# ScalarE's order in the second layer of a fused convolution and gated MLP

## The chip, the cores and the metric

The kernel runs on one core of one Trainium2 chip. The metric is the device time of one execution in microseconds (us), given as the median of several runs. The engines are named as in the profile: PE is TensorE (matmuls; its weight loads are listed as PEld), ACT is ScalarE, DVE is VectorE, POOL is GpSimd, and SP is the engine that only issues DMAs here.

## The reference, cut to what matters

```python
def _attn_ref(x, weight):                      # x: 8 x 4096 x 192, weight: 8 heads x 7 taps
    w = softmax(weight)                        # over the 7 taps
    x_pad = np.concatenate([np.zeros((B, 6, D)), x], axis=1)
    x_unf = x_pad[:, idx, :].reshape(B, S, K, H, group)
    return np.einsum('hk,bskhg->bshg', w, x_unf).reshape(B, S, D)

def _moe_ref(x, w_in, w_out):                  # 32768 x 192, 192 x 2048, 2048 x 192
    h = x @ w_in
    g = h * np.clip(h + 3.0, 0.0, 6.0) / 6.0
    return g @ w_out
```

The result y of the convolution goes through the first layer (`x @ w_in`), the gate, and the second layer (`g @ w_out`). All is float32.

## The kernel before, in words

**Blocks.** The 32768 tokens are cut into 32 blocks (NB) of 1024, each of two halves of 512. Block 0 is done in a plainer way beside the preparation of the weights. Blocks 1 to 31 run in a loop (lines 1116 to 1134): `first_layer(i)`, then `second_layer(i)`. Beside the second layer of block i the kernel prepares the next blocks: it loads x of block i+2, starts its convolution (two of the seven taps), and splits y of block i+1 into three parts that the first layer reads: `split_high` (ACT, line 476), `split_low` (DVE, line 1081), `split_mix` (DVE, line 479). The parts are then swapped between the two halves of the partitions by six DMAs on POOL's queue (`swap_parts`, lines 266 and 267).

**Second layer as seven products.** The gated values `g` are held as a 2x2 matrix of blocks (A11, A21, A12, A22) and `w_out` as B11 to B22. The product is formed by Strassen's scheme in Winograd's form: seven products P1 to P7 of sums of A blocks (S1 to S4) and of B blocks (T1 to T4), which are then added up. In two of the three output thirds of some products the same scheme is used once more on quarters ("level two", `small` and `level_two`), with matmuls of 256 columns instead of 512.

**Four streams.** A matmul here uses 32 of PE's 128 columns. Four streams (j = 0 to 3), one for each group of 32 columns and so for the 32 partitions `rows(j)` of PSUM, run side by side. Each stream is a list of matmuls laid on a clock by hand (`put`): a matmul of 512 columns costs 2 steps, one of 256 costs 1 step, and every stream ends at step 80 (line 814). All other work of the layer is put on the same clock by `do(t, ...)`: a job with time t is written out after all matmuls that begin by then. At the end all jobs and matmuls are sorted by their times and issued in that order (line 910). So the times fix only the order on each engine, in which the engine then works strictly; what a job waits for is found by the framework, which adds the semaphores.

**What the streams hold.** Stream 3 (fourth column group) is made of 56 matmuls of 256 columns (level two of P1 and of P5) and 12 of 512: four of P2 and eight that `fill` puts in, P5's third third into rows 96 to 127 of the PSUM bank b. `fill` runs at steps 4, 36, 48 and 76. Stream 0 holds P4's third third (steps 0 to 16, into `b[first]`, rows 0 to 31), later at step 44 P6 on top of P1 in the same bank, and at step 64 P3.

**The jobs that the change and the prediction touch**, all inside `second_layer`:

- `p4[third, t]` <- `b[first, t]` (lines 816, 817): ACT copies P4's third third out of PSUM in two halves of 256 columns. In the trace these are L650 COPY `shared<-psum` 32x256 x2.
- `b[m]` <- `p1` (line 848): ACT writes P1 into PSUM bank b, where P6 is then added to it by matmuls: P1's seed. In the trace: L650 COPY `psum<-z` 96x512.
- `negative(pair)` (lines 713, 714 and 851, 852): S4 = A12 - S2 for two of the eight chunks, four pairs in all. ACT writes -S2 into S3's place (L572 ACTIVATE `s<-g`), then POOL issues a DMA that adds A12 to it in memory (`adding`, line 569, `s<-g`). P3 reads the pairs (0,2), (1,3), (4,6), (5,7) at steps 64, 68, 72 and 76. A fifth job of the same kind, `last_sum`, writes into `sums2` (`z<-z`).
- `split_high` (put at 48.4, line 1126): the rounding of y, L476 ACTIVATE `y_own<-y`. `split_low` (57) reads it.
- `late["p7"]` <- `c[m]` (line 853, at 56.5), then on DVE `late["u3"]` = `b[m]` + `late["p7"]` (line 854, at 60.2; L458). The add reads bank b before P3 overwrites it at step 64.

Of the kernel before, what the change touches and what calls it, by code (L numbers as in the profile page):

```python
# [25 lines left out]
def kernel(  # L26
# [61 lines left out]
    for base, dma in ((0, nc.scalar), (D2, nc.sync)):  # L88
        dma.dma_start(  # L89
            out=w_sb[base : base + D2],  # L90
            in_=weight.unsqueeze(1).to_broadcast([H, GJ, KC]),
# [126 lines left out]
    for n in range(AHEAD):  # L218
# [8 lines left out]
        out=e_sb[:], in0=w_sb[:], in1=mx[:].to_broadcast([P, KC]), op=ALU.subtract  # L227
# [53 lines left out]
    def take():  # L281
        return free_banks.pop(0)
# [163 lines left out]
    def rows(q):  # L446
        return slice(q * QS, (q + 1) * QS)
# [20 lines left out]
    m = slice(0, DH)  # L468
# [116 lines left out]
    chunk_pairs = [slice(n, n + 3, 2) for n in (0, 1, 4, 5)]  # L585
# [35 lines left out]
    def second_layer(i, between):  # L621
        last = i + 1 == NB
        ours = [free_slots.pop(0) for _ in range(3)]
        x_, b, y_, c, a, _ = (psum[:, 2 * n + k] for n in ours for k in range(2))
        z = pools[1].tile([P, NP + 1, N], F32, name="z2", tag="other")
        sums2, p1 = z[:, 0:NP], z[0:DH, NP]
        ends = [psum[:, 2 * free_slots[0] + k] for k in range(2)] if last else [b, b]
        s5 = A22
        copy = nc.scalar.copy
        m = slice(0, DH)  # L630
        lo, hi = halves
        both = nc.sync, nc.scalar
        first, second, third, fourth = (rows(q) for q in range(4))
# [15 lines left out]
        def do(t, fn, *args, **kw):  # L649
            streams[3].append((t - 0.5, lambda: fn(*args, **kw)))  # L650
# [87 lines left out]
        p4 = Fourth()  # L738
# [75 lines left out]
        assert clock == [80] * 4  # L814

        for t in halves:
            do(35.1 if t == hi else 35, copy, out=p4[third, t], in_=b[first, t])
        do(25.5, copy, out=p1[third], in_=b[second])
        do(20, copy, out=B2, in_=A2)
        do(31.9, copy, out=C2, in_=B2)  # L820
# [24 lines left out]
        do(36.15, small_sums, s5, S1, (3,), nc.vector)  # L845
        do(36.2, small_sums, s5, S1, (2,), nc.vector)
        do(36.05, fold_with, p4, 2)
        do(40 if last else 38.7, copy, out=b[m], in_=p1)
        do(21, last_sum, sums2, A12)
        do(36.4, small_sums, s5, S1, (1, 4), nc.vector)  # L850
        for r, t in zip(chunk_pairs, (30.5, 39.7, 42.1, 48.3)):
            do(t, negative, r)
        do(56.5, lambda: copy(out=late["p7"], in_=c[m]))
        do(60.2, lambda: add(late["u3"], b[m], late["p7"]))
# [83 lines left out]
    with tc.manual_schedule():  # L938
# [4 lines left out]
            out=c_sb[:], in0=e_sb[:], in1=sm[:].to_broadcast([P, KC]), op=ALU.mult  # L943
# [14 lines left out]
        b = take()  # L958
        for _ in range(3):

            nc.tensor.matmul(
                out=psum[:, b], lhsT=zeros[:, 0:P], rhs=zeros[:], start=True, stop=True
# [59 lines left out]
        for slot, (c, group) in enumerate(parts):  # L1022
            first = slot < len(early)
# [88 lines left out]
        last = ctx.enter_context(tc.tile_pool(name="last", bufs=1, reuse_waits="tile"))  # L1112
# [3 lines left out]
        for i in range(1, NB):  # L1116
            jobs = {n: [tap] for n, tap in zip((-1, 1, 3, 5, 7), taps)}
            jobs[-1] = left + jobs.get(-1, [])
            first_layer(i, jobs)
            def begin_conv():  # L1120
                x_tiles[i + 2] = load_x(i + 2)
                conv[:] = conv_jobs(i + 2)

            between, conv = [], []
            if i + 1 < NB:
                between += [(48.4, split_high), (57, split_low), (70, split_mix)]
                between += [
                    (t, lambda n=n: swap_parts(nc.gpsimd, (n,)))
                    for n, t in ((HIGH, 69), (LOW, 69), (MIX, 71))
                ]  # L1130
            if i + 2 < NB:
                between += [(1, begin_conv), (61.5, lambda: conv[0]()), (62, lambda: conv[1]())]
            left = second_layer(i, between)
            taps = conv[2:]
# [33 lines left out]
```

## Time and profile before

| | |
|---|---|
| median of 3 runs | 2226.67 us (2226.42 to 2227.29) |
| the profiled execution's own time | 2226.7 us |
| its span in the trace | 2224.9 us |
| busy: PE, DVE, ACT, POOL | 100%, 89%, 78%, 53% of the span |
| granted PE clock over the span | 0.999 |
| first layer, block 3 (168.06 to 201.03 us) | 32.97 us: PE 32.97, DVE 29.92, ACT 30.97, POOL 23.93 busy |
| second layer, block 3 (201.03 to 236.40 us) | 35.37 us: PE 35.37, DVE 31.69, ACT 23.28, POOL 13.29 busy |

How to read it: the span runs from the first to the last instruction in the trace, and the execution's own time is 1.8 us longer. The busy time of PE is a union of matmul records, which overlap in time and whose ends are modelled, so that PE can be named busy while one of the four streams stands still. Each float32 matmul of the second layer shows as two records, one behind the other in the same column group.

### The profile page before, as it was taken

Reading aid. Unit: us, or ns where it says so; the run is one execution under the profiler, and the core shown is the slowest. Engines: PE = TensorE matmul, PEld = TensorE weight load, DVE = VectorE, ACT = ScalarE, POOL = GpSimd, SP = SyncE. Lnnn points to the kernel's source line nnn. Section 1 sums busy time; section 2 is a strip of 40 time slices with the busy share of each in tenths; the row PEclk is TensorE's granted clock in tenths of the full one; section 3 lists DMA queues with packets and bytes.
Section 4 is the critical chain, followed back from the end, with each engine's and each line's share of the span. In section 5 each row is a group of like instructions: output and inputs, shape, how many; then the busy total and the mean of one; then the engine's idle time right before and its main releaser. Section 6 shows DMA issues by size and latency. Waiting matters only on the chain.

```text
span 2224.9 us, 55392 instructions
## 1 busy us (share of the span) xinstructions
PE 2216.5 (100%) x22984; PEld 1516.6 (68%) x22984; DVE 1985.6 (89%) x1983; ACT 1738.1 (78%) x2391; POOL 1182.2 (53%) x1033
## 2 busy tenths in 40 slices
PE   9999999999999999999999999999999999999998
PEld 5467776677766676766777667776667776677766
DVE  8889998889898899988999988989889998899877
ACT  7478787787877878877878778787787887787876
POOL 2456644565544565445655456554456644556544
PEclk9999999999999999999999999999999999999999
DMA  6277778777778777787777877777877778777777
GB/s 157 61 135 144 144 145 150 138 142 146 144 137 160 134 144 138 145 155 131 143 148 144 145 145 141 146 140 143 155 135 144 138 148 153 132 144 144 132 140 119
DMA packets 353308, 313.20 MB, mean 141 GB/s; under 512 B 212480, under 2 KB 265216, under 8 KB 353056
## 3 DMA queue, kind: packets, MB, share of 16 engines
q0 software_dynamic: 114976, 234.46, 58.8%
q1 hardware_dynamic: 236840, 74.93, 16.7%
q8 instruction: 180, 2.95, 0.6%
q14 instruction: 72, 0.59, 0.1%
q10 hardware_dynamic: 1240, 0.27, 0.1%
HBM read 31.72 MB, written 25.17 MB: 26 GB/s over the span
## 4 chain that ended last, share of the span: by engine, by line
PE 99%; DVE 0%; ACT 0%; DMA 0%; SPq 0%; issue 0%; DVEq 0%; ACTq 0%
PE psum L653 49%; PE psum L511 46%; PE psum L296 2%; PE psum L341 2%; DMA x<-in_x_dram 0%; DVE shared L458 0%; DVE shared L464 0%; SPq L100 0%; SPq L133 0%; DVE top L175 0%; PE psum L953 0%; DVE y L255 0%; SPq L89 0%; ACT y L967 0%; ACT scale L186 0%
## 5 line engine op out<-in xcount | busy, mean ns | idle before, releaser
L653 PE MATMUL psum<-g,w_out 128*32 128x512 f32 (+1 forms) x5968 | 825.0, 503 | 0.3 <-ACT psum L650 0.3
L653 PE MATMUL psum<-s,w_out 128*32 128x512 f32 (+1 forms) x3024 | 710.5, 586 | 0.0
L306 DVE SCALAR_TENSOR_TENSOR g<-g,psum 128x1024 f32<-128x1024 f32 (+1 forms) x528 | 618.7, 1185 | 91.4 <-ACT g L302 90.8
L302 ACT ACTIVATE g<-psum,half 128x1024 f32<-128x1024 f32 (+1 forms) x528 | 565.2, 1087 | 6.0 <-PE psum L511 5.1
L653 PEld LDWEIGHTS psum<-g,w_out 128*32 128x32 f32 x5968 | 370.8, 110 | 254.5 <-issue 91.6
L511 PE MATMUL psum<-y_own,w_in 64*128 64x512 f32 x4464 | 523.3, 389 | 0.0
L511 PE MATMUL psum<-y_other,w_in 64*128 64x512 f32 x4464 | 516.0, 386 | 0.0
L523 ACT ACTIVATE psum<-psum 128x1024 f32<-128x1024 f32 x465 | 468.7, 1008 | 48.1 <-PE psum L511 45.5
L511 PEld LDWEIGHTS psum<-y_own,w_in 64*128 64x128 f32 x4464 | 413.5, 184 | 117.7 <-issue 26.0
L511 PEld LDWEIGHTS psum<-y_other,w_in 64*128 64x128 f32 x4464 | 418.1, 184 | 87.8
L603 POOL TENSOR_TENSOR shared<-g,shared 128x256 f32<-128x256 f32 x248 | 357.6, 1442 | 72.6 <-DVE g L306 41.4
L1058 DVE SCALAR_TENSOR_TENSOR y<-x,c_sb,y 128x1536 f32<-128x1536 f32 x186 | 335.3, 1803 | 1.5 <-ACT y L1056 1.4
L569 POOL DMA_DIRECT2D s<-g x124 | 148.4, 1197 | 283.5 <-ACT s L572 282.6
L653 PE MATMUL psum<-g,w_s 128*32 128x256 f32 x1488 | 287.0, 379 | 0.0
L653 PEld LDWEIGHTS psum<-s,w_out 128*32 128x32 f32 x3024 | 198.4, 110 | 77.3 <-issue 16.2
L569 POOL DMA_DIRECT2D g<-g x124 | 181.7, 1530 | 104.4 <-DVE s L414 104.4
L653 PE MATMUL psum<-z,w_out 128*32 128x256 f32 x992 | 232.8, 380 | 0.0
L653 PE MATMUL psum<-z,w_s 128*32 128x256 f32 x992 | 227.5, 379 | 0.0
L603 POOL TENSOR_TENSOR shared<-g 128x256 f32<-128x256 f32 x124 | 92.0, 742 | 166.8 <-DVE g L306 166.8
L266 POOL DMA_DIRECT2D y_other<-y_own x90 | 47.9, 532 | 238.3 <-PE psum L653 223.6
L650 ACT COPY psum<-psum 32x512 f32<-32x512 f32 x186 | 82.9, 446 | 116.7 <-PE psum L653 113.7
L653 PEld LDWEIGHTS psum<-g,w_s 128*32 128x32 f32 x1488 | 135.3, 110 | 52.7
(115 smaller groups left out, 2970.0 us busy)
## 6 DMA issues: line engine op xcount, KB each, us to landing
y_other<-y_own POOLq DMA_DIRECT2D x180, 384.0 KB, 8.1
g<-g POOLq DMA_DIRECT2D x124, 512.0 KB, 6.1
s<-g POOLq DMA_DIRECT2D x124, 512.0 KB, 6.7
z<-g POOLq DMA_DIRECT2D x62, 512.0 KB, 7.5
out_dram<-shared SPq DMA_DIRECT2D x378, 64.0 KB, 4.1
x<-in_x_dram SPq DMA_DIRECT2D x53, 388.5 KB, 5.7
z<-g SPq DMA_DIRECT2D x31, 512.0 KB, 3.3
stage<-in_moe_w_in_dram SPq DMA_DIRECT2D x16, 192.0 KB, 4.3
```

The costliest lines, as they stand in the source:

```text
L266: dma.dma_start(out=to[D2:P], in_=part[0:D2])
L296: nc.tensor.matmul(out=psum[:, b], lhsT=w[r], rhs=src, start=start, stop=stop, skip_group_check=onto,)
L302: nc.scalar.activation(r6, h, ACT.Relu, bias=half[:], scale=1.0 / 6.0)
L306: nc.vector.scalar_tensor_tensor(out=g_, in0=g_, scalar=1.0, in1=h, op0=ALU.min, op1=ALU.mult)
L341: lambda p=p: nc.tensor.matmul(out=bank[j * QS : (j + 1) * QS, tokens], lhsT=w_out[:, p, w, cols], rhs=x[:, p, tokens], start=(first and p ...
L511: nc.tensor.matmul(out=psum[:, 2 * slots[n] + k], lhsT=r32(w_in_parts[part][r, c, s]), rhs=r32(y_other[0][r, part, s] if group else y_own[ ...
L523: nc.scalar.mul(both(n), both(n), 4097.0)
L569: nc.gpsimd.dma_start(out=out, in_=x, accum_op=ALU.add)
L603: engine.tensor_tensor(out=o, in0=p, in1=q, op=op)
L650: streams[3].append((t - 0.5, lambda: fn(*args, **kw)))
L653: nc.tensor.matmul(out=out, lhsT=w, rhs=x, start=start, stop=True, tile_position=(0, j * QS), skip_group_check=True,)
L1058: jobs.append(lambda k=k: nc.vector.scalar_tensor_tensor(out=y[:], in0=x[:, :, k : k + N], scalar=c_sb[:, k : k + 1], in1=y[:], op0=ALU.mu ...
```

## The change

Two sets of times on the hand-laid clock are altered; no instruction is added or taken away.

```diff
         for t in halves:
-            do(35.1 if t == hi else 35, copy, out=p4[third, t], in_=b[first, t])
+            do(30 if t == hi else 29, copy, out=p4[third, t], in_=b[first, t])
         do(25.5, copy, out=p1[third], in_=b[second])
...
-        do(40 if last else 38.7, copy, out=b[m], in_=p1)
+        do(39.55 if last else 38.7, copy, out=b[m], in_=p1)
         do(21, last_sum, sums2, A12)
         do(36.4, small_sums, s5, S1, (1, 4), nc.vector)
-        for r, t in zip(chunk_pairs, (30.5, 39.7, 42.1, 48.3)):
+        for r, t in zip(chunk_pairs, (34.3, 36.3, 42.1, 52)):
             do(t, negative, r)
```

On ACT the order of a block (all but the last) becomes as follows; what is not named keeps its place.

| before | after |
|---|---|
| L744, **negation (0,2)**, L650 (256), L650 (512), **P4's two copies**, L748 x2, **seed**, L744, L650, **negation (1,3)**, L824, negation (4,6), L826, L827, L743, L650, **negation (5,7)**, **rounding of y**, L745, L853 (P7) | L744, **P4's two copies**, L650 (256), L650 (512), **negation (0,2)**, L748 x2, **negation (1,3)**, **seed**, L744, L650, L824, negation (4,6), L826, L827, L743, L650, **rounding of y**, **negation (5,7)**, L745, L853 (P7) |

In the last block there is no rounding of y: there negation (1,3) and the seed move ahead of L650 and L824, and negation (5,7) moves behind L745. The orders on PE, DVE, POOL and SP are the same as before. One wait of PE moves: the second `fill` (step 36) waited for the second of P4's copies; now only the P2 matmul at step 40 behind it has a wait for ACT there, for the copy L650 (512).

## The prediction, made before the changed kernel was run

> **What bounds the kernel now.** I read the chain of waits first, then PE's starts inside one second layer, then ACT and DVE beside them. The chain of waits names PE for 99% of the span and repeats every 68.33 us (lines from block 2 and 3, columns start, us, what):
>
> ```profile
> PE 99%; DVE 0%; ACT 0%; DMA 0%; SPq 0%; issue 0%; DVEq 0%; ACTq 0%
> ```
>
> ```profile
> 168.06 32.98 PE psum L511 x288
> 201.03 35.37 PE psum L653 x293
> 236.40 32.97 PE psum L511 x288
> ```
>
> That PE is busy without a gap does not mean that its streams are. In the second layer the starts of one stream's records show its pace: 0.429 us for 512 columns (234.90, 235.33, 235.76) and 0.216 us for 256 (228.27, 228.49). The timeline of PE in block 3 breaks that pace twice (start, us, what, xcount):
>
> ```profile
> 216.45 0.66 PE L653 MATMUL psum<-s,w_out 128*32 128x512 f32 x2
> 216.66 0.38 PE L653 MATMUL psum<-z,w_out 128*32 128x256 f32 x1
> 216.88 0.66 PE L653 MATMUL psum<-s,w_out 128*32 128x512 f32 x2
> 217.06 0.62 PE L653 MATMUL psum<-g,w_out 128*32 128x512 f32 x1
> ...
> 228.49 0.81 PE L653 MATMUL psum<-g,w_out 128*32 128x256 f32 x3
> 229.30 0.63 PE L653 MATMUL psum<-s,w_out 128*32 128x512 f32 x3
> 229.32 0.62 PE L653 MATMUL psum<-g,w_s 128*32 128x256 f32 x2
> ```
>
> Hold A: the `g` record at 217.06 is the second `fill` of stream 3. The last `shared` record of that stream began at 216.31, so it was due at 216.53: stream 3 is 0.53 late. Streams 1 and 2 (the `s` records) go on at their pace. Hold B: at 229.30 all four streams begin together, at P3 (step 64), while the ones that were on time (start 228.05, 0.43 long) had been done at 228.48. The list of waits says what ended each (us in total, times, longest):
>
> ```profile
> PEld psum L653 <- DVE shared L458: 14.3, 30, 0.5
> PEld psum L653 <- ACT shared L650: 13.1, 31, 0.4
> ```
>
> Each comes once per block: A is P4's copies, B is the add u3, which must read bank b before P3 overwrites it. Who made these late is in the timelines of ACT and DVE:
>
> ```profile
> 214.36 1.05 ACT L572 ACTIVATE s<-g 128x1024 f32<-128x1024 f32 x1
> 215.44 0.92 ACT L650 COPY psum<-psum 32x256 f32<-32x256 f32 x2
> 216.38 0.62 ACT L650 COPY shared<-psum 32x256 f32<-32x256 f32 x2
> 217.03 0.37 ACT L748 COPY z<-psum 32x256 f32<-32x256 f32 x1
> ...
> 219.00 0.59 ACT L650 COPY psum<-z 96x512 f32<-96x512 f32 x1 [1.22 <-PE psum L653]
> ...
> 224.29 1.06 ACT L572 ACTIVATE s<-g 128x1024 f32<-128x1024 f32 x1
> 225.26 1.48 ACT L476 ACTIVATE y_own<-y 128x1536 fp32r<-128x1536 f32 x1
> ```
>
> ```profile
> 226.77 1.76 DVE L1081 TENSOR_TENSOR y_own<-y,y_own 128x1536 fp32r<-128x1536 f32 x1 [1.82 <-ACT y_own L476]
> ...
> 228.56 0.69 DVE L458 TENSOR_TENSOR shared<-psum,shared 96x512 f32<-96x512 f32 x1
> ```
>
> P4's copies stand behind a negation; ACT then idles 1.22 us ahead of the seed, and from 219.00 on works without a pause up to the rounding of y, for which DVE idles 1.82 us; split_low and u3 follow on DVE back to back, and B ends with u3 at 229.25.
>
> **The change part by part.** No work is added or removed, and POOL's DMAs keep their order, so only places count. I lay ACT's new order out with its own rows; the spacing of one to the next is 1.08 for a negation, 0.65 for P4's two copies, 0.94 for the two L650, 0.77 for the two L748, 0.52 for the seed, 0.97 for L476 behind a negation, 1.50 behind L476.
>
> *P4's copies to steps 29 and 30.* They start at 214.36 and end at 215.0 instead of 217.00; their input was complete at step 16. `fill`, due at 216.53, is no longer held: hold A goes (0.53 of stream 3). The two L650 then run 215.01 to 215.95, earlier than before.
>
> *Negations (0,2) and (1,3) ahead of the seed.* (0,2) starts at 215.95, L748 at 217.03 as before, (1,3) at 217.80, the seed at 218.88 instead of 219.00. The seed waited for PE's `fill`, whose last record ends 0.53 earlier without A (218.43), so ACT sets it now; it ends at 219.47, and P6 needs it at step 44, 200.98 + 44 x 0.429 = 219.87 (0.02 for the slow first record). The cover is 0.40 us; each us beyond it would be one for all streams. The 1.08 of (1,3) now fills ACT's idle 1.22 us: all behind the seed is earlier by 1.08 + 0.12 = 1.20. POOL gets (0,2) at 217.05 instead of 215.71, (1,3) at 218.9 instead of 221.53, so neither is near its need at steps 64 and 68 (228.45, 230.17): landing takes 5.0 to 9.0 us over the span.
>
> *Rounding of y ahead of negation (5,7).* L476 starts at 224.29 - 1.20 = 223.09 instead of 225.26 and ends at 224.57. DVE is busy until 224.95 with rows that wait for nothing here, so split_low starts at 224.97 and ends at 226.73. P7's copy: (5,7) from 224.60, L745 at 225.57, L853 at 225.95 to 226.5. So u3 runs 226.75 to 227.45, against a need at step 64 of 200.98 + 64 x 0.429 = 228.45: hold B goes with 1.0 us to spare.
>
> *What is late next.* (5,7) ends on ACT at 225.65 and goes to POOL then, as before (225.65); P3 reads it at step 76, 233.6. The four landings of this block took 5.0 to 7.3, the longest for one right behind another; in the new order the four are issued at about 217.05, 218.9, 221.5 and 225.7 and overlap less, so I take 5.9 (the median of the four in this block) and a landing at 231.6, with bounds from 5.0 to the longest of the whole span, 9.0 (230.7 to 234.7). Only beyond 7.9 would PE wait. What follows split_low and u3 on DVE and ACT (L1056, L1058, the add of P2 for which y_other's swaps on POOL wait) moves forward with them. DVE itself has 31.69 us of work in the layer, 2.9 less than its new length.
>
> One price hangs on POOL's issue, 1.20 us beside an idle DVE for (5,7) and now beside split_low. The issues of `g<-g` took up to 2.25 us; 1.05 more is the bound above (the landings of 5.0 to 9.0 are counted from the issue's start and hold such issues too), 1.18 the one below. I take 1.20, the row of the same instruction (beside DVE's L458 at 221.53 it also took 1.20).
>
> *The sum.* With no hold, stream 3 sets the end of the layer: 56 matmuls of 256 and 12 of 512, two records each: 112 x 0.2158 + 24 x 0.4292 = 34.47 us (the paces to four digits, from the starts of single records). To this come 0.02 for the slow first record and 0.09 between the streams' end and the first L511 (236.33 - 235.81 - 0.43): 34.58. Now it is 236.33 - 200.96 = 35.37. Gain 0.79 per block; I take 0.77, for a second slow restart somewhere. It is not A plus B: stream 3's lateness of A ends inside B, so A alone would bring nothing, and B alone only what lies between stream 3's late end (228.49 + 3 x 0.216 = 229.14) and 229.30. For 30 blocks: 23.1 us. In the last block the chain leaves PE once more: the seed, behind L824 and negation (1,3), holds all streams until 2202.68. Due was (first record of that layer at 2182.68) 2182.68 + 0.02 + 44 x 0.429 = 2201.58; the new order gives the seed at about 2200.95 to 2201.55, so 1.1 less 0.1 for stream 3's slower pace, which the restart no longer hides: 1.0. Together 24.1.
>
> From the span: 2224.9 - 24.1 = 2200.8, and 1.8 around it (2226.7 - 2224.9) gives 2202.6; the profiled execution stands at the runs' median (2226.67). I say 2203.
>
> **The rivals.**
>
> *One hold stays, or a smaller one takes its place.* The seed's cover is the thinnest, 0.40 us, and it is the end of nine ACT jobs in a row (214.36 to 219.47). For it: ACT has no pause there any more. Against it: each job's inputs were done before its new time ((0,2)'s S2 at 213.6, (1,3)'s at 215.4). If the seed comes 0.8 us later than I have it, PE loses 0.4 a block, 30 x 0.4 = 12: 2215.
>
> *The last pair (5,7) lands too late: slower.* It is the only negation that keeps its old time while PE, faster by 0.77, reaches it earlier. Place: P3 at step 76, 233.6. From a landing time of 7.9 us PE waits, from 7.9 + 0.77 = 8.7 the block is longer than before. At 9.0 it would be 225.7 + 9.0 - 233.6 = 1.1 of waiting less 0.77, 30 x 0.33 = 10 us more: 2237. For it: 9.0 is in the view of these DMAs. Against it: the four were at most 7.3 in this block, and they were closer together than they will be.
>
> *Nothing moves:* the streams' late starts are made good somewhere else, for example in the first layer, where ACT is busy 30.97 of 32.97 us. Then 2226.7. For it: PE is busy 35.37 of 35.37 us. Against it: PE's records in the first layer follow each other at 0.227 us without a hold, and the starts above show streams standing while PE counts as busy. [...]
>
> **How the numbers follow.** My forecast has 0.80 (2200 to 2208); one hold staying 0.11 (2208 to 2221); no change 0.03; slower 0.06. I call a difference measurable from 0.2%, 4.5 us (2222.2 to 2231.1). So faster 0.91, same 0.03, slower 0.06. Range: 2200 (all of 0.79 and 1.1, less a little) to 2214 with most of the first rival in it; the last pair's upper bound stays outside.
>
> **What would show it.** The waits PEld L653 <- ACT shared L650 and <- DVE shared L458 should be gone, the second layer 34.6 us instead of 35.37, the first unchanged at 32.97; DVE's 1.82 us ahead of L1081 near zero; L476 22.1 us after the layer's first record instead of 24.3; ACT without the 1.22 us ahead of the seed. Wrong would be a new wait of PE for `psum` L650 (the seed) or for the DMA `s<-g`, or a first layer that has grown.

## The result and the profile after

The changed kernel takes 2204.11 us (median of 4 runs, 2203.68 to 2204.38), the kernel before 2226.94 us on the same chip (2226.42 to 2227.29): a ratio of 0.9897, with a 95% interval of 0.988 to 0.9915. 2203.0 us was predicted. The profiled span is 2201.9 us instead of 2224.9.

The chain of waits of the changed kernel (start, us, what) repeats every 67.58 us:

```profile
132.83 34.61 PE psum L653 x289
167.44 32.97 PE psum L511 x288
200.41 34.61 PE psum L653 x289
235.02 32.97 PE psum L511 x288
```

The second layer went from 35.37 to 34.61 us; the first kept its 32.97. From the first second layer in the loop to the last, the mean period went from 68.335 to 67.580 us, so 0.755 a block, 22.6 for 30 blocks.

The list of PE's waits after (us in total, times, longest); the two lines of hold A and hold B are gone from it:

```profile
PEld psum L653 <- issue: 123.4, 460, 0.4
PEld psum L341 <- issue: 28.6, 94, 0.8
PEld psum L511 <- issue: 26.0, 31, 0.8
PEld psum L511 <- ACT psum L523: 6.8, 30, 0.2
```

The timeline of ACT in block 3, whose first L653 record starts at 200.34 (before: 200.96):

```profile
213.86 0.62 ACT L650 COPY shared<-psum 32x256 f32<-32x256 f32 x2
214.51 0.91 ACT L650 COPY psum<-psum 32x256 f32<-32x256 f32 x2
215.45 1.06 ACT L572 ACTIVATE s<-g 128x1024 f32<-128x1024 f32 x1
...
217.19 1.05 ACT L572 ACTIVATE s<-g 128x1024 f32<-128x1024 f32 x1
218.27 0.58 ACT L650 COPY psum<-z 96x512 f32<-96x512 f32 x1
...
222.59 1.50 ACT L476 ACTIVATE y_own<-y 128x1536 fp32r<-128x1536 f32 x1
223.98 1.04 ACT L572 ACTIVATE s<-g 128x1024 f32<-128x1024 f32 x1
```

P4's copies come first, the 1.22 us of idle ahead of the seed are filled with negation (1,3), and the rounding starts 22.25 us after the layer's first record instead of 24.30. DVE beside it:

```profile
224.38 1.75 DVE L1081 TENSOR_TENSOR y_own<-y,y_own 128x1536 fp32r<-128x1536 f32 x1
226.47 0.69 DVE L458 TENSOR_TENSOR shared<-psum,shared 96x512 f32<-96x512 f32 x1 [0.34 <-PE psum L653]
```

`split_low` no longer waits for ACT; the add u3 now waits 0.34 us for PE, so the dependence has turned round, and it ends at 227.16, 0.67 us before its need at step 64 (200.34 + 0.02 + 64 x 0.4292 = 227.83).

In the last block two waits are new, which the list of waits of that stretch shows (2155 us to the end):

```profile
PEld psum L653 <- ACT shared L744: 0.8, 1, 0.8
PEld psum L653 <- DMA s<-g: 0.3, 1, 0.3
```

### The profile page after: what moved, and what is told of

It is laid out like the page before. It is cut to its first block, busy times and chain, and to the rows that moved or that the text cites. A ratio compares the mean times of both kernels' runs of the same rounds, so it can differ in the third digit from the quotient of the medians.

```text
span 2201.9 us, 55361 instructions
## 1 busy us (share of the span) xinstructions
PE 2193.5 (100%) x22984; PEld 1564.6 (71%) x22984; DVE 1983.1 (90%) x1983; ACT 1738.8 (79%) x2391; POOL 1181.4 (54%) x1033
## 4 chain that ended last, share of the span: by engine, by line
PE 99%; DVE 0%; DMA 0%; SPq 0%; ACT 0%; issue 0%; DVEq 0%; ACTq 0%
PE psum L653 49%; PE psum L511 46%; PE psum L296 2%; PE psum L341 2%; DMA x<-in_x_dram 0%; DVE shared L458 0%; SPq L100 0%; DVE shared L464 0%; SPq L133 0%; DVE top L175 0%; PE psum L953 0%; DVE y L255 0%; SPq L89 0%; ACT y L967 0%; ACT scale L186 0%
## 5 line engine op out<-in xcount | busy, mean ns | idle before, releaser
L653 PE MATMUL psum<-g,w_out 128*32 128x512 f32 (+1 forms) x5968 | 824.2, 503 | 0.0
L306 DVE SCALAR_TENSOR_TENSOR g<-g,psum 128x1024 f32<-128x1024 f32 (+1 forms) x528 | 619.2, 1186 | 108.3 <-ACT g L302 107.9
L653 PE MATMUL psum<-s,w_out 128*32 128x512 f32 (+1 forms) x3024 | 712.1, 585 | 0.0
L653 PEld LDWEIGHTS psum<-g,w_out 128*32 128x32 f32 x5968 | 382.1, 110 | 221.9 <-issue 112.2
L511 PE MATMUL psum<-y_own,w_in 64*128 64x512 f32 x4464 | 523.3, 389 | 0.0
L511 PE MATMUL psum<-y_other,w_in 64*128 64x512 f32 x4464 | 516.0, 386 | 0.0
L523 ACT ACTIVATE psum<-psum 128x1024 f32<-128x1024 f32 x465 | 468.7, 1008 | 48.3 <-PE psum L511 46.2
L511 PEld LDWEIGHTS psum<-y_own,w_in 64*128 64x128 f32 x4464 | 413.5, 184 | 117.6 <-issue 26.0
L511 PEld LDWEIGHTS psum<-y_other,w_in 64*128 64x128 f32 x4464 | 418.1, 184 | 87.8
L653 PE MATMUL psum<-g,w_s 128*32 128x256 f32 x1488 | 284.5, 379 | 0.0
L653 PEld LDWEIGHTS psum<-s,w_out 128*32 128x32 f32 x3024 | 231.8, 110 | 34.5 <-issue 11.2
L653 PE MATMUL psum<-z,w_s 128*32 128x256 f32 x992 | 227.7, 379 | 0.0
L653 PE MATMUL psum<-z,w_out 128*32 128x256 f32 x992 | 227.0, 379 | 0.0
L650 ACT COPY psum<-psum 32x512 f32<-32x512 f32 x186 | 82.9, 446 | 116.1 <-PE psum L653 113.2
L458 DVE TENSOR_TENSOR g<-g 128x1024 f32<-128x1024 f32 x124 | 149.4, 1221 | 19.3 <-PE psum L653 17.1
L653 PEld LDWEIGHTS psum<-g,w_s 128*32 128x32 f32 x1488 | 137.8, 110 | 38.1
```

The lines of the kernel that those rows point to most:

```text
L306: nc.vector.scalar_tensor_tensor(out=g_, in0=g_, scalar=1.0, in1=h, op0=ALU.min, op1=ALU.mult)
L458: nc.vector.tensor_tensor(out=out, in0=x, in1=y, op=op)
L511: nc.tensor.matmul(out=psum[:, 2 * slots[n] + k], lhsT=r32(w_in_parts[part][r, c, s]), rhs=r32(y_other[0][r, part, s] if group else y_own[ ...
L523: nc.scalar.mul(both(n), both(n), 4097.0)
L653: nc.tensor.matmul(out=out, lhsT=w, rhs=x, start=start, stop=True, tile_position=(0, j * QS), skip_group_check=True,)
```

## The experiments

Diffs are against the kernel named in each heading. The period is the mean time from one second layer of the loop to the next. Where the fill is called late, its lateness is the start of the second `fill` (step 36) after the layer's first record, less the 15.57 us of the changed kernel; in the kernel before it is 0.53.

| kernel | median us | ratio to before (95%) | period, us |
|---|---|---|---|
| changed | 2204.11 | 0.9897 (0.988 to 0.9915) | 67.58 |
| e1: P4's copies alone | 2214.55 | 0.9943 (0.9928 to 0.9958) | 67.92 |
| e2: (5,7) behind the rounding alone | 2220.77 | 0.9971 (0.996 to 0.9982) | 68.14 |
| e3: the two negations alone | 2237.25 | 1.0045 (1.0028 to 1.0062) | 68.67 |
| e4: all but P4's copies | 2237.3 | 1.0045 (1.003 to 1.006) | 68.67 |
| e5: all but (5,7) | 2204.2 | 0.9898 (0.9883 to 0.9913) | 67.58 |
| e6: all but the two negations | 2207.82 | 0.9915 (0.9899 to 0.9932) | 67.70 |
| e7: rounding ahead of the seed | 2242.13 | 1.0069 (1.0054 to 1.0084) | 68.85 |
| e8: (5,7) behind P7's copy | 2204.16 | 0.9898 (0.9884 to 0.9913) | 67.58 |
| e9: (5,7) behind L1056 | 2272.8 | 1.0209 (1.0192 to 1.0226) | 69.87 |
| e10: last block, (1,3) behind the seed | 2203.88 | 0.9898 (0.9883 to 0.9913) | 67.58 |
| e11: first scaling split | 2218.24 | 0.9962 (0.9948 to 0.9976) | 68.08 |
| e12: last block, two moves | 2204.0 | 0.9897 (0.9881 to 0.9914) | 67.58 |

### e1: P4's copies alone (against the kernel before)

```diff
-            do(35.1 if t == hi else 35, copy, out=p4[third, t], in_=b[first, t])
+            do(30 if t == hi else 29, copy, out=p4[third, t], in_=b[first, t])
```

> The kernel before with one edit: P4's two copies at steps 29 and 30; negations, seed and rounding keep their places. As the prediction has it (stream 3's lateness ends inside hold B, so A alone brings nothing): the block stays at 68.33 us, the time within 1 us of 2226.9. Rival, the chain theory: the seed waits for PE's fill, which A made late, and ACT works without a pause from the seed to the rounding of y, so the 0.53 us that A took from the fill come back at hold B as well: the seed starts about 0.5 us earlier, PE's wait for the copies is gone, the one for u3 stays at 30 times, the second layer takes about 34.85 us, and the time is 2226.9 - 30 x 0.53 = 2211.

It gained 0.42 us a block, 12.7 in all, so the prediction's "A alone would bring nothing" is wrong. The seed and the restart of P3 in block 3, whose first record starts at 200.59:

```profile
218.21 0.58 ACT L650 COPY psum<-z 96x512 f32<-96x512 f32 x1 [0.68 <-PE psum L653]
228.50 0.63 PE L653 MATMUL psum<-s,w_out 128*32 128x512 f32 x3
```

After the layer's first record the seed started at 17.62 us instead of 18.04 and P3 restarted at 27.91 instead of 28.34: hold B moved by just as much as the seed did. The wait for u3 is still there 30 times. That it was 0.42 and not 0.53 has a cause of its own. PE in block 3, a little earlier, and its waits over the whole span:

```profile
215.64 0.60 PE L653 MATMUL psum<-s,w_out 128*32 128x512 f32 x2
215.71 0.38 PE L653 MATMUL psum<-z,w_out 128*32 128x256 f32 x1
215.72 0.38 PE L653 MATMUL psum<-shared,w_out 128*32 128x256 f32 x1
215.93 0.38 PE L653 MATMUL psum<-z,w_out 128*32 128x256 f32 x1
215.94 0.38 PE L653 MATMUL psum<-shared,w_out 128*32 128x256 f32 x1
216.23 0.40 PE L653 MATMUL psum<-z,w_out 128*32 128x256 f32 x1
216.24 0.62 PE L653 MATMUL psum<-s,w_out 128*32 128x512 f32 x2
216.25 0.62 PE L653 MATMUL psum<-g,w_out 128*32 128x512 f32 x1
```

```profile
PEld psum L653 <- DVE shared L458: 14.8, 30, 0.5
PEld psum L653 <- ACT psum L650: 13.4, 32, 1.2
```

Negation (0,2), still early, now stands between P4's copies and L650, for whose result stream 0 waits at step 36 (216.23). The `s` streams were due at 215.64 + 0.43 = 216.07 and began at 216.24; stream 3 was due at 215.94 + 0.216 = 216.16 and began at 216.25. All four began within 0.02 us of each other (216.23 to 216.25): one stream's wait held all four here, and 0.1 of hold A came back. In hold A of the kernel before, stream 0, due at 216.66 + 0.216 = 216.88, began with the fill at 217.06 too; streams 1 and 2 lost nothing: they had begun matmuls of two records each at 216.45, and their next ones were due only at 217.31, after the fill's release (217.06).

### e2: negation (5,7) behind the rounding alone (against the kernel before)

```diff
-        for r, t in zip(chunk_pairs, (30.5, 39.7, 42.1, 48.3)):
+        for r, t in zip(chunk_pairs, (30.5, 39.7, 42.1, 52)):
```

> The kernel before with one edit: negation (5,7) behind the rounding of y. Hold A stays (PE's wait for ACT's copies, 30 times). The rounding starts about 1.06 us earlier, u3 with it, and PE's wait for u3 goes or shrinks below 0.1 us. By the prediction's sum a layer with A alone ends where stream 3's lateness puts it, 0.16 us earlier, up to 0.26 by the starts of the trace: 2226.9 - 30 x 0.16 to 0.26 = 2219 to 2222. Rival: if hold A costs nothing while B is there and nothing once B is gone, the time is that of the whole change, 2204.

Hold B went, hold A stayed (PE's wait for `shared` L650: 13.1 us, 31 times). The fill is 0.52 us late, and stream 3 carries that to the end of the layer: 34.61 + 0.52 = 35.13 against 35.165 measured. 0.20 us a block, as expected.

### e3 and e4: without P4's copies in their new place

e3 against the kernel before, e4 against the changed kernel:

```diff
-        do(40 if last else 38.7, copy, out=b[m], in_=p1)
+        do(39.55 if last else 38.7, copy, out=b[m], in_=p1)
-        for r, t in zip(chunk_pairs, (30.5, 39.7, 42.1, 48.3)):
+        for r, t in zip(chunk_pairs, (34.3, 36.3, 42.1, 48.3)):
```

```diff
-            do(30 if t == hi else 29, copy, out=p4[third, t], in_=b[first, t])
+            do(35.1 if t == hi else 35, copy, out=p4[third, t], in_=b[first, t])
```

> The kernel before with one edit: negation (0,2) behind the two L650 copies, (1,3) ahead of the seed; P4's copies and the rounding keep their places. If the parts are independent, the 1.2 us idle ahead of the seed is filled, hold B goes as in the whole change, hold A stays: 2219 to 2222. Rival, the parts hang together: without P4's copies there, ACT comes to the L650 copies too early and waits for PE, (0,2) then stands between them and P4's copies, the fill is held by about 1.1 us instead of 0.53, the seed ends about 0.2 us past its need at step 44, the second layer takes 35.4 to 35.7 us, and the time is 2227 to 2236, no faster than before.

> The changed kernel with P4's copies back at steps 35 and 35.1. Independent parts: only hold A comes back, 2219 to 2222. Rival, the parts hang together: the copies stand behind the two L650, which wait for PE, and behind negation (0,2); the fill is held by about 1.1 us and stream 3 sets the layer's end, with or without hold B: 35.4 to 35.7 us, 2227 to 2236.

Both are slower than the kernel before, by the same amount, though e4 holds two of the three moves. ACT in e3, block 3:

```profile
215.30 0.91 ACT L650 COPY psum<-psum 32x256 f32<-32x256 f32 x2 [0.54 <-PE psum L653]
216.14 1.05 ACT L572 ACTIVATE s<-g 128x1024 f32<-128x1024 f32 x1
217.22 0.62 ACT L650 COPY shared<-psum 32x256 f32<-32x256 f32 x2
```

ACT reaches L650 0.54 us too early, waits for PE, and P4's copies stand behind that wait and the negation. The fill is 1.06 us late (16.63): 34.61 + 1.06 = 35.67 against 35.703 measured. The parts hang together: P4's copies must go first for the negation's new place to pay.

### e5 and e6: one part back (against the changed kernel)

```diff
-        for r, t in zip(chunk_pairs, (34.3, 36.3, 42.1, 52)):
+        for r, t in zip(chunk_pairs, (34.3, 36.3, 42.1, 48.3)):
```

```diff
-        do(39.55 if last else 38.7, copy, out=b[m], in_=p1)
+        do(40 if last else 38.7, copy, out=b[m], in_=p1)
-        for r, t in zip(chunk_pairs, (34.3, 36.3, 42.1, 52)):
+        for r, t in zip(chunk_pairs, (30.5, 39.7, 42.1, 52)):
```

> The changed kernel with negation (5,7) back ahead of the rounding of y. In the changed kernel's trace u3 ended 0.67 us before its need at step 64 and had waited 0.34 us for PE besides. With (5,7) ahead, the rounding starts about 1.0 us later, at 223.6, the two vector jobs behind it end at about 227.5, need 227.83: no hold, 2204 (the move of the rounding is spare). Rival, the prediction's cover of 1.0 us, less 1.08 for a negation, gives a hold of 0.1 us, up to 0.25 with the slow restart: 2207 to 2211.

> The changed kernel with negations (0,2) and (1,3) and the seed of the last block back in their old places; P4's copies and the rounding moved. With P4's copies alone, negation (0,2) stood between them and the first L650 copy, which held PE at step 36 and made stream 3 0.10 us late. Theory: that 0.10 stays and nothing else, since the rounding behind (1,3) but ahead of (5,7) is early enough: layer 34.7 us, 2204.1 + 30 x 0.10 = 2207, with up to 0.6 more in the last block. Rival, each of the three parts is needed: hold B comes back in part, 2212 or more.

e5: the move of (5,7) brings nothing once the other two are there. u3 ends at 227.49, 27.19 us after the first record, 0.30 before its need at step 64. e6: 0.12 us a block, and it isn't hold B: the wait for u3 is gone from its list, and the one for `psum` L650 (13.4 us, 32 times) is that of e1, at step 36. So either of the two moves takes hold B away; what the negations add to the rest is that (0,2) no longer stands ahead of L650.

### e7: the point from which the seed decides (against the changed kernel)

```diff
-                between += [(48.4, split_high), (57, split_low), (70, split_mix)]
+                between += [(36.45, split_high), (57, split_low), (70, split_mix)]
```

> The changed kernel with the rounding of y (1.5 us) moved ahead of the seed, behind negation (1,3). By the prediction's cover of 0.40 us for the seed: the seed ends about 1.45 us later, PE waits for it (psum L650) at step 44 by about 1.05 us in every block but the last, and all streams with it: 2204 + 30 x 1.05 = 2236, slower than the kernel before. Rival, the cover is larger than read, or the lateness is made good later in the layer: 2204 to 2215.

The sign and the place are as expected, the size is 1.27 us a block instead of 1.05. PE at the seed in block 3, and the wait over the span:

```profile
220.34 0.38 PE L653 MATMUL psum<-z,w_s 128*32 128x256 f32 x1
220.34 0.38 PE L653 MATMUL psum<-g,w_out 128*32 128x256 f32 x1
221.57 1.49 PE L653 MATMUL psum<-g,w_out 128*32 128x512 f32 x13 [0.78 <-ACT psum L650]
```

```profile
PEld psum L653 <- ACT psum L650: 39.7, 30, 1.3
```

Single records (the line above packs 13) put the first three restarts at 221.57 to 221.58, about 1.0 after the due 220.55, but stream 3's at 221.87, 1.30 after its due. It is stream 3 that sets the end. Why it restarted 0.29 behind the others is open; after hold B of the kernel before it was 0.02.

### e8 and e9: the last pair later, within its cover and past it (against the changed kernel)

```diff
-        for r, t in zip(chunk_pairs, (34.3, 36.3, 42.1, 52)):
+        for r, t in zip(chunk_pairs, (34.3, 36.3, 42.1, 52 if last else 56.6)):
```

e9 has 61.6 in place of 56.6.

> The changed kernel with negation (5,7) at 56.6, behind P7's copy, in all blocks but the last. It ends on ACT about 1 us later, at 226.0, and its DMA lands at about 231.9, or 232.9 if POOL's issue is late too; P3 reads it at step 76, 232.98. Theory: within the cover of 2.1 us that the changed kernel's trace shows, no wait for s<-g: 2204. Rival of the late pair, with the longest landing of 9.0: 235.0, PE waits 2.0 us a block: 2264.

> The changed kernel with negation (5,7) at 61.6, behind L1056, in all blocks but the last. It ends on ACT at about 229.3, 4.3 us later than in the changed kernel, POOL issues it at about 229.5, and with the 5.6 us that the last pair took in the runs so far it lands at 235.1, 2.1 past its need at step 76 (232.98). Theory of the late pair: PE waits for the DMA s<-g by 2.0 to 2.2 us in each of 30 blocks: 2264 to 2270, slower than before. Rival: the lateness of a pair that only one product reads is made good within the last four steps or in the first layer: 2204 to 2240.

Step 76 is due 32.64 us after the layer's first record. The changed kernel's last pair lands 30.55 after it in block 3 (at 230.89), 2.09 us before the need; over the 30 blocks of the loop it lands at 30.52 to 32.10, so the thinnest cover is 0.54. In e8 it lands 1.67 us later in block 3, at 32.22, and the time is the same. In two of e8's 30 blocks, with landings at 32.64 and 32.70, PE waits for it (0.5 us together), and even these layers keep their 34.61 us. In e9 PE waits for it in every block:

```profile
PEld psum L653 <- DMA s<-g: 68.5, 31, 4.0
```

19 of the 30 layers of e9 took 36.23 to 36.43 us, at least 1.62 longer than without the wait; the rest are longer still, up to 40.07, because the landing took 5.12 to 7.24 us (and for a reason told in the last section, which also helps to put the time above the 2264 to 2270 us expected). This is the rival's mechanism, real from the step that the prediction gave: e8's latest landings lie at it, e9's earliest, 34.33, 1.69 us past it. The change stays 0.54 to 2.12 us short of it.

### e10 and e12: the last block (against the changed kernel)

```diff
-        for r, t in zip(chunk_pairs, (34.3, 36.3, 42.1, 52)):
+        for r, t in zip(chunk_pairs, (34.3, 39.7 if last else 36.3, 42.1, 52)):
```

```diff
-        for r, t in zip(chunk_pairs, (34.3, 36.3, 42.1, 52)):
+        for r, t in zip(chunk_pairs, (34.3, 39.5 if last else 36.3, 42.1, 48.3 if last else 52)):
```

> The changed kernel with negation (1,3) back at step 39.7 in the last block only. In the changed kernel's last block PE waited 0.8 us for ACT's copy L744 (z), which stood behind that negation; the block brought 0.50 us instead of the predicted 1.0. Theory: with the negation behind the seed again that wait is gone and the block is 0.5 us shorter: 2203.6, a difference near what 5 rounds can tell, so the verdict is the trace's (no wait for L744, span 0.5 less). Rival: the seed, then behind less work, or the pair (1,3), landing later, holds PE there by as much: span within 0.1 us.

> The changed kernel with two moves in the last block only: L744 ahead of negation (1,3), which stays ahead of the seed, and negation (5,7) ahead of L745. In the runs so far PE waited there for L744 (behind (1,3)), for the DMA s<-g (where (5,7) stood behind L745), or for L743 (where (1,3) stood behind the seed), and the stretch from the first to the last L653 record of that block took 35.3 us in the kernel before and in the changed one alike. Theory: those waits are what ate the 1.0 us that the prediction gave to the last block; without them the stretch is 34.5 to 34.8 us and the time 0.5 to 0.8 below the changed kernel's, 2203.3 to 2203.6, which the trace must tell, since it is below what timing resolves. Rival: another copy on ScalarE is late in their place, and the stretch stays at 35.3.

From the first to the last L653 record of the last block it takes 35.36 us in the kernel before, 35.33 in the changed one, 35.85 in e10 and 35.15 in e12. Each order only changes what PE waits for: in e10 L743 (0.9) and the DMA `s<-g` (0.8), in e12:

```profile
PEld psum L653 <- DMA s<-g: 0.8, 1, 0.8
PEld psum L653 <- ACT psum L743: 0.2, 1, 0.2
```

L744 is no longer waited for, but PE then reaches the pair (5,7) earlier and waits there. Counted from that layer's first record, the pair was issued 1.62 us earlier in e12 than in the changed kernel (23.72 against 25.34) and landed only 0.18 earlier (30.96 against 31.14). Neither theory holds in full: a fifth of a microsecond came of it, below what the runs' times can tell.

### e11: what is left at the start of the first layer (against the changed kernel)

```diff
-            if n + 1 < count:
+            if 0 < n < count - 1:
```

> The changed kernel with one edit outside the change: the first scaling of the first layer is split between ACT and DVE as its last one is. It looks at what is left: PE waits 30 times, 6.8 us in all, for L523 at the first layer's start, and that layer takes 32.97 us. If that wait costs its length: up to 0.08 us a block, 2201.7 to 2203. If DVE, busy at 89% and more, delivers its half later than ACT would: 2204 or slower.

Slower by 14 us. PE's wait for ACT's L523 gives way to one for DVE, `PEld psum L511 <- DVE g L306`, 21.3 us in 29 times, and the first layer grows by 0.5 us to 33.47. DVE after the start of the first layer at 235.33:

```profile
237.05 0.70 DVE L527 TENSOR_SCALAR psum<-psum 128x512 f32<-128x512 f32 x1 [0.87 <-PE psum L511]
...
242.15 2.35 DVE L306 SCALAR_TENSOR_TENSOR g<-g,psum 128x1024 f32<-128x1024 f32 x2
```

Its half of the scaling (L527) stands idle for PE's matmuls for 0.87 us. The adds and transposes left from the second layer, which DVE did in that time in the changed kernel, come behind it, and behind them the gate L306, which starts 6.82 us after the first layer instead of 5.24. PE waits for the gate at 243.42, 8 us into that layer.

## Why the prediction was right, and where it was not

**Holds A and B** went, as said, and no hold took their place inside the loop. The seed's cover was put at 0.40 us and is 0.39 (it ends at 218.85, needed at 219.24); e7 shows that it counts. The rounding was put 22.1 us after the first record and stands at 22.25. u3 has 0.67 us of cover instead of 1.0, because it waits 0.34 for PE, which doesn't delay anything. The last pair took 5.57 us to land in block 3 and 5.91 in the median of the loop, for 5.9 assumed; the longest, 7.11, stays below the 7.9 from which PE would wait.

**The sum per block** was 34.58 us without a hold, a gain of 0.79, taken as 0.77; measured are 34.61 and 0.755. That stream 3 sets the end then is shown by e2, e3 and e4, where its lateness alone gives the layer's length to 0.04 us.

**The last block** is the mis-sized term: 1.0 us was given to it. From first to last L653 record it gained 0.04 us, since the wait for the seed was replaced by those for L744, which stood behind the moved negation (1,3), and for the moved last pair. The prediction counted only the seed's wait and not what PE would meet behind it. The stretch from there to the end was 0.46 us shorter in the changed kernel's profile, but that is scatter: from the first record of that layer to the end it took 41.74 us, and e7, e8, e9 and e11, with the same code there, took 41.73, 42.24, 42.30 and 41.54, against 42.24 in the kernel before. The rest of the difference to the span, 0.12, is a later start of the loop. 22.64 + 0.50 - 0.12 = 23.0 for the 24.1 predicted. So the forecast's closeness, 1.1 us, rests on the sum per block; the 0.46 that seems to bear out half of the last term is luck.

**"A alone would bring nothing"** failed. The prediction took the release of hold B as a fixed time and set stream 3's lateness beside it. But the seed waits for the fill, and ACT works from the seed to the rounding without a pause, so B's release follows the fill; e1 shows both 0.42 to 0.43 us earlier. "B alone 0.16" was nearly right (0.20, e2). Neither touched the forecast, in which both go.

**The move of (5,7)** was counted as what takes B away. By the prediction's own rows it wasn't needed: with everything behind the seed 1.20 us earlier and (5,7) left ahead of the rounding, u3 ends at 229.25 - 1.20 = 228.05, 0.40 us before its need at 228.45. The prediction didn't work this out; e5 measures 0.30.

**The rivals.** Both holds that could have come up are real: a seed about 1.0 us past its cover cost 1.27 us a block (e7), and a pair landing at least 1.69 us past its need cost 1.62 us or more (e9). The seed's price was put too low, at 1 us for each us, and what stream 3 adds to it is open. The changed kernel stays below both limits. "Nothing moves" is refuted: PE is busy for 100% of the span in both profiles, and the span is 23 us shorter.

## What to carry to other kernels

Before adding up holds, follow who releases each: a hold whose releaser waits in turn for a stream that an earlier hold delayed moves with it, so parts that look separate can be worth more alone, nothing, or less than nothing. Give each moved job the slack to its need, in the order in which the engine reaches it, and look at the last block by itself: another order there exchanged one wait for the next. A job moved in front of another also moves the wait that it meets: the two negations alone made the kernel 10.0 us slower (e3).

## What the runs showed of the hardware

In e9 a long pause of PE cost more than itself. Its windows (us, PE busy, PEld, DVE, ACT, POOL, granted PE clock, DMA share, GB/s) around the wait in block 3, which ends at 237.73:

```profile
235.31:238.72 3.41, 0.99 (x12) 0.39 (x16) 1.53 (x3) 0.00 (x0) 2.01 (x4) 1.00 0.99 227
238.72:242.13 3.41, 3.41 (x20) 1.48 (x14) 0.96 (x2) 0.58 (x1) 0.00 (x0) 0.50 1.02 290
242.13:245.54 3.41, 3.41 (x32) 2.69 (x32) 3.34 (x4) 2.25 (x3) 0.00 (x0) 1.00 0.99 266
```

PE had stood for 2.86 us. One microsecond after the restart the granted clock fell to 0.50 and stayed there for 3.41 us; the records of 512 columns took 1.09 us instead of 0.61. Four of the 30 waits met such a slow stretch, with pauses of 2.43, 2.65, 2.86 and 3.50 us; one of 2.61 and all 25 up to 2.41 us did not. So the length of the pause alone doesn't decide.

The slow stretches begin at 238.72, 1283.20, 1426.56 and 1638.18 us, and the times between them are 306, 42 and 62 times 3.413 us, so in this run the drops lie on one beat, at no fixed distance from a pause. (At 1283.20 that was 0.9 us before the restart, and the stretch lasted two beats, 6.83 us.) In the beat just before each drop PE was busy for only 0.82 to 1.25 us of 3.41. The pause of 2.61 us, from 1070.93 to 1073.54, lay across two beats, of which the emptier still had 1.45 us of matmuls; of all the beats of the loop without a drop behind them, none had less:

```profile
1071.57:1074.98 3.41, 1.45 (x16) 0.42 (x16) 1.33 (x3) 0.00 (x0) 1.82 (x4) 1.00 1.04 216
1074.98:1078.40 3.42, 3.42 (x34) 2.37 (x28) 2.14 (x4) 1.59 (x2) 0.00 (x0) 1.00 1.05 255
```

So in this run a drop followed beats with 0.82 to 1.25 us of matmuls and none with 1.45 us or more; what decides between the two is not shown.

The DMA of the last pair took longer to land the closer it was issued behind the one ahead of it. That third one was issued 20.9 us after the layer's first record and landed at 27.9 to 28.0 in e5, the changed kernel, e8 and e9 (medians of the loop). The last was issued 2.7, 4.0, 5.6 and 8.3 us behind it, and took 7.3, 5.9, 5.3 and 5.2 us. So e5, which issues it 1.37 us earlier than the changed kernel, has it landed no earlier, at 30.90 against 30.89. Why is open.
